# New SBUF addresses for three kinds of tiles in a fused attention, MLP and routed-expert kernel

## The chip, the cores and the metric

The kernel runs on one core of a Trainium2 chip. The metric is the device time of one execution in microseconds (us); lower is better. Matrix products run on TensorE (PE in the profile; its weight loads are the row PEld), which computes in turn with VectorE (DVE), ScalarE (ACT) and GpSimd (POOL); SyncE (SP) issues most transfers.

## The reference

Three stages follow one another, all in float32.

```
phi(x):  proj = x @ w_phi; proj -= max|proj|;  concat(exp(proj), exp(-proj))
attn  = (phi(q) @ (phi(k)^T v)) / (phi(q) @ sum phi(k) + 1e-6)    # 8 x 8 heads, 576 tokens, 64
x     = attn as 4608 tokens x 512
h     = x @ w_in;  x = (h * cos(h)) @ w_out                       # 512 -> 2048 -> 512
e     = argmax(x @ w_gate + modality_bias[modality_id]); p = its softmax weight
out   = p * (relu(x @ w1[e]) @ w2[e])                             # 8 experts, 512 -> 1024 -> 512
```

## The kernel before

**Attention** (lines 54 to 280) goes through 16 items of two batches by two heads, five groups each. Its products are L136 (projection), L174 (keys by values, the moving operand `v`) and L210 (numerator and denominator).

**The MLP** takes the tokens in 9 blocks `u` of 512 and, in each, 16 steps `f` of 128 hidden features. Each float32 operand is split into a high and a low part in the fp32r type, and a product is three matmuls (high by high, high by low, low by high). Step `f` issues 12 matmuls of 512 columns for the first layer (L473: stationary a 128x128 piece of the chunk `w0_f`, moving the tokens `x`) and then, three steps behind, 12 for the second (L511: stationary `gh` or `gl`, moving the chunk `w1_(f-3)`; in the last two blocks L516, with the roles exchanged). So steps 0, 1 and 2 of a block hold the second layer's chunks 13, 14 and 15 of the block before. The work around it is the cosine on ACT and DVE.

**The experts** take the sorted tokens in 18 slots of 256 and, after these, up to seven half slots of 128 (`half`, L799). A slot is 96 matmuls of 256 columns (L781: stationary the weight chunks `m0_f`, moving the turned tokens `xT_i`), then 48 of 512 columns (L793: stationary `hh` or `hl`, moving `m1_f` in even and `m2_f` in odd slots: 24 for each half of the tokens, three for each chunk `f`). In between lie transposes for the next slot (L766).

**Where tiles lie.** Tile pools are laid out one behind the other in each partition. The pool of the shared tiles (`SHARED`, a dictionary of floats per tile and number of tiles) comes early, then the pool `m_small` with the small tiles of routing and planning, then what lives in the attention alone; when the attention ends, the pool `late` takes that last place. `late` holds the 11 weight chunks that have no shared tile (tag `wl`, 4096 bytes each) and the tiles `x1T`. A chunk is a pair of halves, high and low, of 512 floats each, made by `pair`. The late chunks are `w0_12` to `w0_15` and `w1_9` to `w1_15`, and in the expert stage, in the same places, `m1_4` to `m1_7` and `m2_1` to `m2_7`. All other chunks, `m0` whole among them, lie in shared tiles.

The address of a tile is here its first byte within each partition, in the built program, and its remainder is that address modulo 512. The order of the work around the change is set by the code's own order and the planner of the tile framework.

Of the kernel before, what the change touches and what calls it, by code (L numbers as in the profile page):

```python
# [14 lines left out]
I32 = mybir.dt.int32  # L15
AF = mybir.ActivationFunctionType
ALU = mybir.AluOpType
AX = mybir.AxisListType
# [12 lines left out]

SHARED = {"raw_k":(1024,2),"raw_q":(1024,2),"ke":(1024,4),"qe":(1024,3),"xT":(1152,4),"xw":(1024,6),"kt":(512,3),"qt":(512,3),"kvh":(512,4),"kvl":(512,4),"kvt":(512,2),"wx":(1024,5),"sx":(1024,2)}

def shared_tiles(tc, ctx):
    sp=ctx.enter_context(tc.tile_pool(name="shared",bufs=1))
    def S(tag,name,dt=F32):
        w,n=SHARED[tag]
        return sp.tile([P,w],dt,tag=tag,name=name,bufs=n)  # L40
# [305 lines left out]
def moes(tc, ctx, consts, S, ps, ident, att, end_att, xt, w_in, w_out, x1d, tab, wgt, w1, w2, out):  # L346

    nc=tc.nc
# [8 lines left out]
    def xtile(tag,name,dt=F32R):  # L357
        if tag=="x1T": return late[0].tile([P,512],dt,tag="x1T",name=name,bufs=4)
        if tag=="row": return S(turn(("kvt","kvt","qt"),tag),name,dt)
        return S({"fr":"kt","n":"qt","gh":"kvh","gl":"kvl"}[tag],name,dt)  # L360
    def pair(tag,name):

        if tag=="wl": t=late[0].tile([P,1024],F32R,tag="wl",name=name,bufs=11)
        else: t=S(tag,name,F32R)
        return t[:,0:512],t[:,512:1024]
    pj=[]
    def bank(tag,name):
        if tag=="pj":
# [34 lines left out]
    def decoding(paced=False,steps=False):  # L403
# [7 lines left out]
        t=xtile("gl" if decoded[0]<=20 else "row",f"d_t{which}_{f}",F32)  # L411
        ti=t.bitcast(I32)
        h,l=pair(wtag[which][f],f"w{which}_{f}")
        (win,wout)[which][f]=(h,l)
        keep=tc.keep_in_program_order if paced else lambda ins: ins
# [43 lines left out]
    def split_x(u,d):  # L459
        if u>=NU: return  # L460
        r=xraw[u,d]
        h,l=pair("ke",f"x_{u}_{d}")
        nc.vector.tensor_copy(h,r)  # L463
        (nc.vector if d==3 else nc.gpsimd).tensor_tensor(l,r,f32(h),ALU.subtract)
        xhl[u,d]=(h,l)
# [62 lines left out]
    def load_gate():  # L528
        for tag in ("raw_k","raw_k","raw_q","kvt","kvt"):
            t=S(tag,f"wg_{len(wg)}")  # L530
            for j in range(SHARED[tag][0]//512):
                e=len(wg)
# [51 lines left out]
    def small(n,u,shape,dt=F32): return sb.tile(shape,dt,tag="s_"+n,name=f"{n}_{u}",bufs=1)  # L584
# [50 lines left out]
    o={}; e_={}; off_={}  # L635
    PRE=4; TAKE=64*T-8
    def key(n):

        t=small(n,0,[1,8])
        nc.vector.tensor_tensor(t,C["run"][0:1,:],C["base"][0:1,:],ALU.subtract)  # L640
        nc.vector.scalar_tensor_tensor(t,t,64.0,C["num"][0:1,:],op0=ALU.mult,op1=ALU.add)
        return t
    def value(ap,engines,hi,why): return nc.values_load(ap,engines=engines,min_val=0,max_val=hi,skip_runtime_bounds_check_because=why)
    SP=[mybir.EngineType.SP]
    def first():

        t0=t=key("k1")
        m=small("km",0,[1,PRE])
        for j in range(PRE):
            nc.vector.tensor_reduce(m[:,j:j+1],t,AX.X,ALU.max)  # L650
            h=small("kis",0,[1,8]); nc.vector.tensor_tensor(h,t,m[:,j:j+1].to_broadcast([1,8]),ALU.is_equal)
            n=small(f"kt{j}",0,[1,8]); nc.vector.scalar_tensor_tensor(n,h,-float(TAKE),t,op0=ALU.mult,op1=ALU.add)
            t=n
        o["took"]=small("took",0,[1,8]); nc.vector.tensor_tensor(o["took"],t,t0,ALU.subtract)
        mi=small("kmi",0,[1,PRE],I32); nc.vector.tensor_copy(mi,m)
        e=small("kme",0,[1,PRE],I32); nc.vector.tensor_scalar(e,mi,7,None,op0=ALU.bitwise_and)
        g=small("kmg",0,[1,PRE],I32); nc.vector.tensor_scalar(g,mi,56,None,op0=ALU.bitwise_and)
        ef=small("kef",0,[1,PRE]); nc.vector.tensor_copy(ef,e)
        gf=small("kgf",0,[1,PRE]); nc.vector.tensor_copy(gf,g)
        nc.vector.tensor_scalar(ef,ef,float(REG),None,op0=ALU.mult)  # L660
        of=small("kof",0,[1,PRE],I32)
        nc.vector.scalar_tensor_tensor(of,gf,T/8.0,ef,op0=ALU.mult,op1=ALU.add)
        o["pe"]=e; o["poff"]=of
    def order():


        t=key("k2")
        nc.vector.tensor_tensor(t,t,o["took"],ALU.add)
        srt=small("srt",0,[1,8]); nc.vector.max(srt,t)
        ki=small("ki",0,[1,8],I32); nc.vector.tensor_copy(ki,srt)  # L670
        ei=small("ei",0,[1,8],I32); nc.vector.tensor_scalar(ei,ki,7,None,op0=ALU.bitwise_and)
        gi=small("gi",0,[1,8],I32); nc.vector.tensor_scalar(gi,ki,56,None,op0=ALU.bitwise_and)
        n=small("on0",0,[1,16])
        for j,more in ((0,T//2-1),(1,T-1)):
            kj=small(f"ki{j}",0,[1,8],I32); nc.vector.tensor_scalar(kj,ki,64*more,None,op0=ALU.add)
            nc.vector.tensor_scalar(kj,kj,14,None,op0=ALU.logical_shift_right)
            nc.vector.tensor_copy(n[:,8*j:8*j+8],kj)
        nc.vector.tensor_tensor(n[:,8:16],n[:,8:16],n[:,0:8],ALU.subtract)

        b=small("ob",0,[1,17]); nc.vector.memset(b[:,16:17],0.0)  # L680
        nc.vector.tensor_scalar(b[:,0:8],ei,8.0*REG+1.0,None,op0=ALU.mult)
        gf=small("gf",0,[1,8]); nc.vector.tensor_copy(gf,gi)
        nc.vector.scalar_tensor_tensor(b[:,0:8],gf,float(T),b[:,0:8],op0=ALU.mult,op1=ALU.add)
        nc.vector.scalar_tensor_tensor(b[:,8:16],n[:,0:8],8.0*T,b[:,0:8],op0=ALU.mult,op1=ALU.add)
        end=small("on1",0,[1,16])
        nc.vector.tensor_tensor_scan(end,C["ones"],n,float(PRE),op0=ALU.mult,op1=ALU.add)
        db=small("db",0,[1,16]); nc.vector.tensor_tensor(db,b[:,1:17],b[:,0:16],ALU.subtract)
        nc.vector.scalar_tensor_tensor(db,n,-8.0*T,db,op0=ALU.mult,op1=ALU.add)
        ge=small("ge",0,[1,NS1,16])
        nc.vector.tensor_tensor(ge,C["slot"].unsqueeze(2).to_broadcast([1,NS1,16]),end.unsqueeze(1).to_broadcast([1,NS1,16]),ALU.is_ge)  # L690
        nc.vector.tensor_tensor(ge,ge,db.unsqueeze(1).to_broadcast([1,NS1,16]),ALU.mult)
        sv=small("sv",0,[1,NS1+8+16])[:,0:NS1]; nc.vector.tensor_reduce(sv,ge,AX.X,ALU.add)
        nc.vector.scalar_tensor_tensor(sv,C["slot"],8.0*T,sv,op0=ALU.mult,op1=ALU.add)
        iv=small("iv",0,[1,NS1],I32); nc.vector.tensor_scalar(iv,sv,b[:,0:1],-8.0*T*PRE,op0=ALU.add,op1=ALU.add)
        ie=small("ie",0,[1,NS1],I32); nc.vector.tensor_scalar(ie,iv,7,None,op0=ALU.bitwise_and)
        io=small("io",0,[1,NS1],I32); nc.vector.tensor_scalar(io,iv,3,None,op0=ALU.logical_shift_right)

        ni=small("ni",0,[1,3+NSH],I32)
        nc.vector.tensor_copy(ni[:,0:1],end[:,7:8]); nc.vector.tensor_copy(ni[:,1:2],end[:,15:16])
        h=small("oh0",0,[1,NSH]); nc.vector.tensor_scalar(h,C["slot"][:,NS0:NS0+NSH],end[:,7:8],None,op0=ALU.is_ge)  # L700
        h2=small("oh1",0,[1,NSH]); nc.vector.tensor_scalar(h2,C["slot"][:,NS0:NS0+NSH],end[:,15:16],None,op0=ALU.is_lt)
        nc.vector.tensor_tensor(ni[:,2:2+NSH],h,h2,ALU.mult)
        h3=small("oh2",0,[1,1]); nc.vector.tensor_scalar(h3,end[:,15:16],NS0+1.5,None,op0=ALU.is_gt)
        nc.vector.scalar_tensor_tensor(ni[:,2+NSH:3+NSH],end[:,7:8],NS0+0.5,h3,op0=ALU.is_lt,op1=ALU.mult)
        o.update(e=ie,off=io,n=ni)
# [5 lines left out]
    def alloc_w():  # L711

        for n in range(NF2):
            tag=wtag[1][n]
            t=late[0].tile([P,1024],F32,tag="wl",name=f"raw_{n}",bufs=11) if tag=="wl" else S(tag,f"raw_{n}",F32)
            RAW.append(t[:,0:1024])
        sets=[[pair(tags[f0+f],f"m{n}_{f}") for f in range(NF2)] for n,(tags,f0) in enumerate(((wtag[0],0),(wtag[0],NF2),(wtag[1],NF2)))]
        for i in range(NS1):
            W[i,0]=sets[0]; W[i,1]=sets[1+i%2]
# [23 lines left out]
    X={}  # L743
    R={}
    def alloc(i):
        X[i]=list(zip(*[pair("ke",f"xT_{i}_{g}") for g in range(2)]))
    xgs={}; spare=[]
    def alloc_g(i):
        R[i]=sb.tile([P,2,2],I32,tag="mrec",name=f"mrec_{i}",bufs=4)
# [141 lines left out]
    for F in range(3,NU*NF+LAG):  # L891
        step(F)
        if F==NF+1: load_gate()
        if F==(NU-1)*NF+3: first()
        if F==(NU-1)*NF+7:
            for i in range(2):
                alloc_g(i); load_off(i); gather(i)
        if F==(NU-1)*NF+11:
            for i in range(3): load_e(i)
            alloc_w()  # L900
            for m in (4,5,6,7,0,1,2,3): fetch(m)
            ws=itertools.chain(split_steps(0,0),split_steps(0,1))
        if F>(NU-1)*NF+12:
            pin.append(1)
            for _ in range(3): next(ws,None)
            pin.pop()
        if F==NU*NF+1: alloc(0); prep(0)
# [7 lines left out]
    def hooks(i,steps):  # L915
# [28 lines left out]
        if i==1:  # L944
            h[1].append(lambda: route2(u))
            h[4].append(order)
# [125 lines left out]
```

## Time and profile before

| | |
|---|---|
| median of 3 runs | 1647.42 us (1645.74 to 1648.21) |
| the profiled execution | 1647.8 us |
| its span, first to last instruction | 1645.6 us |
| PE busy | 1612.9 us, 98% of the span |
| DVE, ACT, POOL busy | 1152.3, 846.9 and 411.0 us |
| moved by DMA | 195.55 MB |

The profiled execution is 2.2 us longer than its span and 0.4 us above the median. Matmuls are pipelined: a matmul's own row shows the time from its start to its modelled end, which overlaps the next one, so what a matmul costs is read from the start of one to the start of the next.

### The profile page before, as it was taken

The numbers are of one execution on the slowest core, as the hardware profiler recorded it, in microseconds if no ns is written. First come the engines' busy times: TensorE is split into PE (matmuls) and PEld (weight loads), VectorE is DVE, ScalarE is ACT, GpSimd is POOL, SyncE is SP. The second block draws the span as 40 slices with busy tenths as digits, with TensorE's granted clock in tenths as the row PEclk, the third lists the DMA queues.
The fourth block names the chain that finished last, engine by engine and source line by source line (L and its number), as shares of the span: only waits on it lengthen the run. The fifth ranks groups of instructions, "written<-read, shape, count | busy, mean of one in ns | idle before, by whom it ended". The sixth has DMA issues, their size and how long they took to land. (4 is left out here: it accounts for less than half of the span.)

```text
span 1645.6 us, 33698 instructions
## 1 busy us (share of the span) xinstructions
PE 1612.9 (98%) x13076; PEld 1375.7 (84%) x13076; DVE 1152.3 (70%) x2364; ACT 846.9 (51%) x1563; POOL 411.0 (25%) x336
## 2 busy tenths in 40 slices
PE   8999999989999999999999999999999999999997
PEld 6888888878788888888888888888899899989985
DVE  5888888888766868586867677665875556565645
ACT  5677666656533434343433333344755555555645
POOL 0000000022123434333333333343112211111113
PEclk9999999999999999999999999999999999999999
DMA  6744444423210101010100101004758667766656
GB/s 170 224 136 137 139 138 140 136 94 125 82 45 14 39 7 45 7 39 14 39 13 21 31 7 39 8 14 146 246 140 314 218 222 244 251 216 214 215 190 234
DMA packets 144832, 195.55 MB, mean 119 GB/s; under 512 B 64648, under 2 KB 89352, under 8 KB 144659
## 3 DMA queue, kind: packets, MB, share of 16 engines
q1 hardware_dynamic: 136866, 172.24, 33.2%
q0 software_dynamic: 7792, 21.02, 3.8%
q8 instruction: 107, 1.75, 0.5%
q14 instruction: 67, 0.54, 0.1%
HBM read 162.18 MB, written 31.82 MB: 118 GB/s over the span
## 5 line engine op out<-in xcount | busy, mean ns | idle before, releaser
L473 PE MATMUL ph<-x,w 128*128 128x512 f32 x1728 | 425.0, 394 | 4.5 <-DVE x L463 3.3
L473 PEld LDWEIGHTS ph<-x,w 128*128 128x128 f32 x1728 | 323.4, 188 | 79.8 <-DVE x L463 4.4
L500 POOL TENSOR_TENSOR gl<-fr,gh 128x512 fp32r<-128x512 f32 x130 | 195.8, 1509 | 367.0 <-DVE gh L499 336.4
L740 DVE TENSOR_TENSOR m<-raw,m 128x512 fp32r<-128x512 f32 x320 | 207.9, 686 | 109.2 <-ACT m L739 109.0
L511 PE MATMUL acc<-w,gh 128*128 128x512 f32 x896 | 277.9, 391 | 0.0
L486 ACT ACTIVATE n<-ph 128x512 int32<-128x512 f32 x144 | 86.0, 597 | 263.7 <-PE ph L473 263.5
L781 PEld LDWEIGHTS mh<-xT,m 128*128 128x128 f32 x1728 | 210.0, 191 | 2.4 <-DVE hl L784 0.7
L781 PE MATMUL mh<-xT,m 128*128 128x256 f32 x1728 | 210.9, 283 | 0.5 <-DVE hl L784 0.5
L739 ACT CAST m<-raw 128x512 fp32r<-128x512 f32 x320 | 187.4, 618 | 42.9 <-PE mh L781 33.6
L511 PEld LDWEIGHTS acc<-w,gh 128*128 128x128 f32 x896 | 168.2, 188 | 36.9
L488 DVE SCALAR_TENSOR_TENSOR fr<-ph,n 128x512 f32<-128x512 f32 x144 | 99.1, 688 | 133.8 <-ACT n L486 117.6
L541 DVE SCALAR_TENSOR_TENSOR junk<-x1T,wg 128x512 f32<-128x512 f32 x224 | 183.0, 817 | 0.0
L793 PE MATMUL po<-m,hh 128*128 128x512 f32 x576 | 182.2, 397 | 0.0
L511 PE MATMUL acc<-w,gl 128*128 128x512 f32 x448 | 175.4, 392 | 0.0
L490 ACT ACTIVATE fr<-fr 128x512 f32<-128x512 f32 x144 | 91.1, 632 | 159.7 <-DVE fr L488 159.5
L493 DVE SCALAR_TENSOR_TENSOR fr<-fr,ph 128x512 f32<-128x512 f32 x144 | 98.6, 684 | 68.6 <-ACT fr L491 68.6
L793 PEld LDWEIGHTS po<-m,hh 128*128 128x128 f32 x576 | 105.5, 188 | 21.7
L793 PE MATMUL po<-m,hl 128*128 128x512 f32 x288 | 113.4, 394 | 0.0
L836 POOL DMA_INDIRECT out_dram<-o,mrec x39 | 42.5, 1089 | 282.3 <-ACT o L835 268.3
L511 PEld LDWEIGHTS acc<-w,gl 128*128 128x128 f32 x448 | 84.1, 188 | 18.5
L491 ACT ACTIVATE fr<-fr 128x512 f32<-128x512 f32 x144 | 90.9, 632 | 4.0
L141 DVE TENSOR_REDUCE m_q<-pj 128x4 f32<-128x512 f32 (+1 forms) x80 | 50.9, 637 | 57.7 <-PE pj L136 57.7
(215 smaller groups left out, 2391.0 us busy)
## 6 DMA issues: line engine op xcount, KB each, us to landing
raw<-in_moe_w_dram SPq DMA_DIRECT2D x170, 512.0 KB, 6.0
xt<-xo SPq DMA_DIRECT2D x16, 576.0 KB, 4.4
xr<-xt SPq DMA_DIRECT2D x36, 256.0 KB, 2.9
raw_k<-in_k_dram SPq DMA_DIRECT2D x32, 256.0 KB, 2.9
raw_q<-in_q_dram SPq DMA_DIRECT2D x32, 256.0 KB, 4.1
v<-in_v_dram SPq DMA_DIRECT2D x64, 128.0 KB, 3.4
st<-in_moe_w_in_dram SPq DMA_DIRECT2D x16, 512.0 KB, 4.1
st<-in_moe_w_out_dram SPq DMA_DIRECT2D x16, 512.0 KB, 3.9
```

The source lines that it names most:

```text
L473: nc.tensor.matmul(ph,A[:,ws],xhl[u,d][k],start=n[0]==0,stop=n[0]==11); n[0]+=1
L488: nc.vector.scalar_tensor_tensor(g,ph,INV2PI,n,op0=ALU.mult,op1=ALU.subtract)
L490: nc.scalar.activation(g,g,AF.Sin,scale=math.pi)
L491: nc.scalar.activation(g,g,AF.Square)
L493: nc.vector.scalar_tensor_tensor(g,g,-0.5,ph,op0=ALU.add,op1=ALU.mult)
L500: nc.gpsimd.tensor_tensor(gl,g,f32(gh),ALU.subtract)
L511: nc.tensor.matmul(accs[u][c],A[:,ws],B,start=(f==0 and k==0),stop=(f==NF-1 and k==2))
L541: return lambda: tc.keep_in_program_order(nc.vector.scalar_tensor_tensor(junk,x1T[u,c],1.0,wg[e],op0=ALU.mult,op1=ALU.mult,accum_out=lgs[u ...
L739: keep(nc.scalar.copy(h,a))
L740: keep(nc.vector.tensor_tensor(l,a,f32(h),ALU.subtract))
L781: nc.tensor.matmul(ph[:,f2*T:(f2+1)*T],A[:,ws],B[d//2][:,xs],start=n==0,stop=n==11); n+=1
L793: nc.tensor.matmul(po[c],A[:,ws],B,start=(f==0 and j==0),stop=(f==NF2-1 and j==2))
```

## The change

Three edits, none of which touches an instruction's kind, size or place.

```diff
-"ke":(1024,4)
+"ke":(1152,4)
...
-    def pair(tag,name):
+    def pair(tag,name,o=0):
...
-        return t[:,0:512],t[:,512:1024]
+        return t[:,o:o+512],t[:,o+512:o+1024]
...
-        e=small("kme",0,[1,PRE],I32); nc.vector.tensor_scalar(e,mi,7,None,op0=ALU.bitwise_and)
-        g=small("kmg",0,[1,PRE],I32); nc.vector.tensor_scalar(g,mi,56,None,op0=ALU.bitwise_and)
+        eg=small("kme",0,[1,2*PRE],I32); e,g=eg[:,0:PRE],eg[:,PRE:2*PRE]
+        nc.vector.tensor_scalar(e,mi,7,None,op0=ALU.bitwise_and)
+        nc.vector.tensor_scalar(g,mi,56,None,op0=ALU.bitwise_and)
...
-        sv=small("sv",0,[1,NS1+8+16])[:,0:NS1]; nc.vector.tensor_reduce(sv,ge,AX.X,ALU.add)
+        sv=small("sv",0,[1,NS1]); nc.vector.tensor_reduce(sv,ge,AX.X,ALU.add)
...
-        X[i]=list(zip(*[pair("ke",f"xT_{i}_{g}") for g in range(2)]))
+        X[i]=list(zip(*[pair("ke",f"xT_{i}_{g}",112) for g in range(2)]))
```

The tiles `ke` grow from 4096 to 4608 bytes, and the turned tokens `xT` begin 448 bytes into them; the MLP's tokens `x`, in the same tiles, still begin at their first byte. Two small tiles of the planning become one, and one loses 24 floats it did not use, which makes `m_small` 128 bytes shorter. The remainders of the addresses in the two built programs:

| tiles | before | after |
|---|---|---|
| shared tiles: chunks `w0_0` to `w0_11`, `w1_0` to `w1_8`, `m0`, `m1_0` to `m1_3`, `m2_0`; `x`, `gh`, `gl`, `hh`, `hl` | 320 | 320 |
| the 11 late chunks | 448 | 320 |
| turned tokens `xT` | 320 | 256 |
| `x1T` (loads of tokens, gathered tokens) | 448 | 320 |
| attention's `v`, in turn | 448, 32 | 320, 416 |
| attention's `qx`, `w2` | 256, 128 | 128, 0 |

The two programs hold the same 21,018 instructions in the same order, with the same waits. The one place where even a name differs is the planning's arithmetic on DVE, in the last block of the MLP (`kme`, `kmg`: the expert's number and its group, cut out of a packed key `kmi`; numbers at the ends of names count tiles):

```order
-L656 TENSOR_SCALAR kme_12391<-kmi_12389 1x4
-L657 TENSOR_SCALAR kmg_12393<-kmi_12389 1x4
+L657 TENSOR_SCALAR kme_12391<-kmi_12389 1x4
+L658 TENSOR_SCALAR kme_12391<-kmi_12389 1x4
 L654 TENSOR_TENSOR took_12387<-kt_0_12385,k_0_12363 1x8
```

Nothing moved there: the second of the two writes goes to the other half of the same tile.

## Rows read from the trace of the kernel before

**Rows 1.** Page, part 1: busy us, share of the span, instructions.

```profile
PE 1612.9 (98%) x13076; PEld 1375.7 (84%) x13076; DVE 1152.3 (70%) x2364; ACT 846.9 (51%) x1563; POOL 411.0 (25%) x336
```

**Rows 2.** Busy time by stage: attention, MLP, expert slots, half slots.

```profile
core 0: us, PE busy (x) PEld busy (x) DVE busy (x) ACT busy (x) POOL busy (x), PEclk, DMA share, GB/s
100.00:330.00 230.00, 223.85 (x4451) 203.71 (x4452) 189.52 (x452) 159.41 (x365) 15.48 (x22) 1.00 0.47 140
400.00:1160.00 760.00, 758.91 (x3407) 617.16 (x3406) 534.25 (x1111) 300.02 (x482) 270.52 (x191) 1.00 0.12 36
1196.10:1596.90 400.80, 400.29 (x2599) 363.67 (x2598) 239.48 (x410) 228.32 (x402) 75.36 (x70) 1.00 0.68 225
1600.00:1645.60 45.60, 36.16 (x172) 28.05 (x170) 25.88 (x42) 27.27 (x51) 14.54 (x7) 0.98 0.64 216
```

**Rows 3.** PE alone, block 4 of the MLP: steps 6 to 9, steps 12 to 15.

```profile
741.62:763.38 21.76, 21.76 (x97) 1.00 0.06 13
774.27:796.61 22.34, 22.34 (x97) 1.00 0.00 1
```

**Rows 4.** Timeline of PE in block 4: steps 2, 3 and 12 (start us, us).

```profile
719.28 2.90 PE L473 MATMUL ph<-x,w 128*128 128x512 f32 x12
722.01 0.62 PE L511 MATMUL acc<-w,gh 128*128 128x512 f32 x2
...
724.81 2.90 PE L473 MATMUL ph<-x,w 128*128 128x512 f32 x12
727.54 0.61 PE L511 MATMUL acc<-w,gh 128*128 128x512 f32 x2
...
730.26 0.20 PE L616 MATMUL pk<-ob,tri 128*128 128x8 bf16 x2
...
774.27 2.96 PE L473 MATMUL ph<-x,w 128*128 128x512 f32 x12
777.06 0.62 PE L511 MATMUL acc<-w,gh 128*128 128x512 f32 x2
...
779.84 2.95 PE L473 MATMUL ph<-x,w 128*128 128x512 f32 x12
```

**Rows 5.** Timeline of PE in expert slots 6 and 7 (start us, us).

```profile
1328.35 0.62 PE L793 MATMUL po<-m,hh 128*128 128x512 f32 x2
...
1331.14 0.63 PE L793 MATMUL po<-m,hh 128*128 128x512 f32 x2
...
1349.77 0.62 PE L793 MATMUL po<-m,hh 128*128 128x512 f32 x2
...
1354.64 0.64 PE L793 MATMUL po<-m,hh 128*128 128x512 f32 x2
```

**Rows 6.** PE alone while L781 runs, in slots 5, 7 and 8.

```profile
1290.55:1302.05 11.50, 11.50 (x97) 1.00 0.58 204
1337.56:1349.07 11.51, 11.51 (x97) 1.00 0.58 204
1361.11:1372.63 11.52, 11.52 (x98) 1.00 0.56 203
```

**Rows 7.** Timeline of PE in the attention: two bursts of L174 and what follows.

```profile
109.72 1.10 PE L174 MATMUL kv<-v,ke 128*64 128x65 f32 x32
110.76 0.44 PE L121 MATMUL pt<-ident,raw_q 128*128 128x128 f32 x2
...
130.59 1.10 PE L174 MATMUL kv<-v,ke 128*64 128x65 f32 x32
131.63 0.65 PE L121 MATMUL pt<-ident,raw_q 128*128 128x128 f32 x4
```

**Rows 8.** Page, part 5: groups of L739, L781, L210 and L136.

```profile
L781 PE MATMUL mh<-xT,m 128*128 128x256 f32 x1728 | 210.9, 283 | 0.5 <-DVE hl L784 0.5
L739 ACT CAST m<-raw 128x512 fp32r<-128x512 f32 x320 | 187.4, 618 | 42.9 <-PE mh L781 33.6 <-DMA raw<-in_moe_w_dram 3.0 <-PE po L793 0.9
L210 PE MATMUL pn<-kvz,qx 128*64 128x65 f32 x2304 | 85.2, 225 | 1.3 <-ACT xo L228 1.3
L136 PE MATMUL pj<-w,qT 64*128 64x128 f32 x576 | 54.6, 300 | 13.1 <-DVE rd L216 8.0 <-DMA w<-in_w_phi_dram 2.2 <-DVE t_k L142 1.4
L136 PE MATMUL pj<-w,kT 64*128 64x128 f32 x576 | 48.0, 276 | 0.0
```

More of the change, by code (lines that the diff above doesn't have):

```diff
@@ L30, in f32 @@
     return ap.bitcast(F32)
-SHARED = {"raw_k":(1024,2),"raw_q":(1024,2),"ke":(1024,4),"qe":(1024,3),"xT":(1152,4),"xw":(1024,6),"kt":(512,3),"qt":(512,3),"kvh":(512,4),"kvl":(512,4),"kvt":(512,2),"wx":(1024,5),"sx":(1024,2)}
+SHARED = {"raw_k":(1024,2),"raw_q":(1024,2),"ke":(1152,4),"qe":(1024,3),"xT":(1152,4),"xw":(1024,6),"kt":(512,3),"qt":(512,3),"kvh":(512,4),"kvl":(512,4),"kvt":(512,2),"wx":(1024,5),"sx":(1024,2)}
 def shared_tiles(tc, ctx):
```

## The prediction

> **What bounds the kernel now.** I read the page's busy times first: PE is busy for 98% of the span, the next engine for 70% [rows 1]. Then the same by stage: in the MLP and in the expert slots PE is busy for all but 1.1 us of 760 and 0.5 us of 401, at a granted clock of 1.00 of 2.4 GHz, while DVE has 70% and 60%, and the transfers take 12% and 68% [rows 2]. So in these two stages the time is the sum of the intervals at which PE starts one matmul after another. Only in the half slots at the end does PE idle, for 9 of 46 us [rows 2]. The change alters no instruction, no order and no wait, so the question is whether an interval depends on where the operands lie.
>
> It does, as the rows stand. Steps 6 to 9 of an MLP block, whose 96 matmuls have all operands at remainder 320, take 21.76 us: 226.7 ns each. Steps 12 to 15 have the same 96 matmuls, but the weight chunks of both layers are late ones at 448, and take 22.34 us: 232.7 ns each [rows 3]. Nothing waits in either: PE is busy for the whole stretch. Two things set the difference apart from the steps around it. In step 2 only the second layer's chunk is late: its half takes 724.81 - 722.01 = 2.80 us, where the first layer's half, from a shared chunk, takes 2.73, and in step 3, where the second layer is back at its chunk 0, its half takes 2.72 [rows 4]. In step 12 both halves are long, 2.79 and 2.78 us [rows 4]. So the extra goes with the chunk, whether it is the stationary operand (L473) or the moving one (L511). The expert slots say the same: 12 matmuls with `m1_4` to `m1_7` take 2.79 us in slot 6, and 21 with `m2_1` to `m2_7` take 4.87 us in slot 7, which is 231.9 ns each [rows 5].
>
> The Trainium skill, "SBUF — State Buffer", section "Who interferes with whom", has it that TensorE reads its moving operand and its weights through two independent ports and never waits on anyone. By that rule no address could matter to PE, and the time would stay. The trace does not agree: 226.7 against 232.7 ns for the same instructions [rows 3].
>
> **The change part by part.**
>
> *Late chunks from 448 to 320, in the MLP.* They come to the remainder that the shared chunks have, so I price their matmuls like those. Steps 12 to 15 give back 22.34 - 21.76 = 0.58 us a block [rows 3]. The second layer's halves of steps 0, 1 and 2 give back 2.80 - 2.72 = 0.08 us each [rows 4], 0.24 in all. That is 0.82 us a block and 7.4 us for nine; in the last two blocks the second layer has its operands exchanged, which I price the same, since both roles show the extra.
>
> *Late chunks in the expert slots.* 12 aligned matmuls cost 12 x 226.7 ns = 2.72 us, and an even slot has two stretches like the one of 2.79 us [rows 5]: 0.14 us. An odd slot has two of 21 matmuls at 4.87 against 4.76 us: 0.22 us. Nine slots of each: 9 x (0.14 + 0.22) = 3.2 us.
>
> *Turned tokens from 320 to 256.* All 1728 matmuls of L781 [rows 8] now read a moving operand 64 bytes off the remainder of their stationary one; until now both were at 320. They cost 11.51 us for 96, or 119.9 ns [rows 6]. No row shows a displacement of 64 bytes in these matmuls. Bounds: 256 more columns cost 226.7 - 119.9 = 106.8 ns, so a matmul of 256 columns has 13.1 ns on top of its columns. If the new place freed all of it, 1728 x 13.1 ns = 22.6 us would go; if it doubled, as much would come. The nearest row is the displacement of 128 bytes, at 232.7 - 226.7 = 6.0 ns: +10.4 us. My value is zero, half-way between these ends: three slots with different token tiles, and with different chunk sets before them, come out within 0.02 us [rows 6], which shows a settled rhythm, and 64 bytes are half of the one displacement whose price is known, in an unknown direction. In the half slots the tokens are stationary and displaced the other way, but PE idles there.
>
> *Everything else.* The tiles `ke` are longer by 512 bytes, which moves all behind them by 2048: remainders there stay. In the attention, `v`, `qx`, `w2` change place. Its L174 has had `v` at 448 and at 32 in turn: bursts of 32 take 1.04 us at 109.72 (448) and 1.04 us at 130.59 (32) [rows 7], so I price the attention at zero. The clock of these rows is 0.01 us, 1%; of the 188 us in L210 and L136 [rows 8], which have no such pair, that is 2 us either way, kept for the range. The planning's arithmetic on DVE has as many instructions as before. The transfers into `x1T` are as large as before, and in the MLP they take 12% of the DMA engines [rows 2]. Where PE gets faster, weights are asked for earlier: ACT's splitting (L739) has waited for weights 3.0 us in all [rows 8], and 0.2 us in a slot of 23.5 is 1% more demand on transfers at 68% [rows 2], so I charge nothing; without that cover the 3.2 us of the expert slots would not come.
>
> The sum is 7.4 + 3.2 = 10.6 us off the profiled execution's 1647.8 us, of which 2.2 lie outside its span. That execution is 0.4 us above the median of the runs, so from 1647.4 the forecast is 1636.8, rounded to 1637.0.
>
> **The rivals.**
>
> *The tokens' new place pays too* (20%). L781 loses part of its 13.1 ns, from 1.5 ns to half of it: 2.6 to 11.3 us more off, 1625.5 to 1634. For it: there is something to lose. Against: equal remainders are the best place that the rows show.
>
> *The tokens' new place costs, but less than the chunks give* (12%). From 1.5 to 6.0 ns, the price of 128 bytes: 1639.5 to 1647.
>
> *Slower: L781 pays a second stall* (5%). If 64 bytes doubled its extra, it would cost 22.6 us against 10.6: 1659.4. It decides from 10.6 us / 1728 = 6.1 ns for no change, and 8.0 ns for slower by over 0.2%. For it: L781 has the shortest matmuls, with a weight load at every 119.9 ns, so a stall has least room. Against: a displacement twice as large costs 6.0 ns.
>
> *It is not the remainder* (8%). The late chunks also lie highest in SBUF, and they come in the same steps each time; if height or neighbours make them slow, the chunks stay at 232 ns and the time stays at 1647.4 (tokens at zero). For it: no row has a late chunk at 320, or a shared one at 448. Against: nothing but PE works differently in step 2's two halves. The ports rule of the Trainium skill, cited above, would end in the same time for another reason.
>
> **How the numbers follow.** The forecast, chunks at 226.7 ns and L781 within 1.5 ns (2.6 us) of now, has 55%: 1634 to 1640. Of the range, the gain on L781 and the attention's 2 us reach down to 1628, the moderate loss up to 1645; outside lie the slower case, "not the remainder" and the far end of the gains, some 18%. A measurement of this kernel can tell about 0.2%, 3.3 us, from no change: faster means below 1644.1. Forecast, gain, and some 8 of the 12 points of the moderate loss lie there: 83%. The other 4 and the 8 of "not the remainder" make the same, 12%; slower is 5%.
>
> **What would show it.** Steps 12 to 15 of a block at 21.76 us instead of 22.34, and step 2's second half at 2.72; `m2_1` to `m2_7` at 4.76 us. L781's 96 matmuls at 11.5 us: at 11.0 the tokens pay, at 12.1 they cost as much as the chunks gave. L174's bursts at 1.04 us. The prediction is wrong if the late chunks stay at 232 ns, or if L781 moves by over 0.4 us a slot.

## The result, and the profile after

The changed kernel takes 1632.36 us (median of 6 runs, 1630.37 to 1635.49) where the kernel before takes 1646.58 (median of 6 runs): a ratio of 0.9917, with a 95% interval of [0.9906, 0.9927]. It is faster, by more than the 10.6 us of the sum. 1632.36 lies 4.6 us below the forecast of 1637.0 and below the 1634 to 1640 that had 55%; it lies within the range of 1628 to 1645, and in the 1625.5 to 1634 of the rival by which the tokens' new place pays too. In the changed kernel every line from 657 on has a number one higher, so L781, L793 and L739 are now L782, L794 and L740.

The page's busy times (part 1) show the same picture as [rows 1], with 14.3 us less of PE:

```profile
PE 1598.6 (98%) x13074; PEld 1370.5 (84%) x13076; DVE 1147.1 (70%) x2364; ACT 846.1 (52%) x1563; POOL 408.5 (25%) x336
```

The windows of the attention, of the MLP and of the expert slots are as full as in [rows 2]; columns as there:

```profile
100.00:330.00 230.00, 223.91 (x4449) 203.57 (x4447) 189.51 (x452) 159.22 (x364) 15.41 (x22) 1.00 0.48 140
400.00:1160.00 760.00, 758.53 (x3433) 620.69 (x3433) 534.16 (x1118) 304.48 (x493) 269.54 (x191) 1.00 0.13 37
1189.03:1582.20 393.17, 392.57 (x2598) 359.42 (x2597) 239.39 (x410) 228.27 (x402) 77.77 (x70) 1.00 0.69 230
```

Now the marks that the prediction set. PE in block 4, steps 6 to 9 and 12 to 15, against [rows 3]:

```profile
738.70:760.46 21.76, 21.76 (x97) 1.00 0.05 13
771.34:793.10 21.76, 21.76 (x97) 1.00 0.00 1
```

The steps with late chunks take what the others take. The timeline of step 2, against [rows 4], shows the second layer's half at 721.90 - 719.18 = 2.72 us:

```profile
719.18 0.62 PE L511 MATMUL acc<-w,gh 128*128 128x512 f32 x2
...
721.90 2.88 PE L473 MATMUL ph<-x,w 128*128 128x512 f32 x12
```

In slot 7, against [rows 5], `m2_1` to `m2_7` take 1344.55 - 1339.79 = 4.76 us:

```profile
1339.79 0.62 PE L794 MATMUL po<-m,hh 128*128 128x512 f32 x2
...
1344.55 0.62 PE L794 MATMUL po<-m,hh 128*128 128x512 f32 x2
```

The tokens' matmuls (L782) in slots 5, 7 and 8, against [rows 6], take 11.31 us for 96, 117.8 ns each, where 11.5 was said:

```profile
1281.63:1292.94 11.31, 11.31 (x98) 1.00 0.63 210
1327.80:1339.11 11.31, 11.31 (x97) 1.00 0.61 212
1350.89:1362.20 11.31, 11.31 (x98) 1.00 0.56 203
```

And a burst of L174, against [rows 7], takes 132.17 - 131.13 = 1.04 us, as before:

```profile
131.13 1.10 PE L174 MATMUL kv<-v,ke 128*64 128x65 f32 x32
132.17 0.66 PE L121 MATMUL pt<-ident,raw_q 128*128 128x128 f32 x4
```

The groups by line, against [rows 8], have L782 at 206.6 us of busy time, 4.3 less than before, and the attention's L210 and L136 within 0.3 us of where they were:

```profile
L782 PE MATMUL mh<-xT,m 128*128 128x256 f32 x1728 | 206.6, 281 | 0.6 <-DVE hl L785 0.6
L740 ACT CAST m<-raw 128x512 fp32r<-128x512 f32 x320 | 187.7, 619 | 39.7 <-PE mh L782 32.5
...
L210 PE MATMUL pn<-kvz,qx 128*64 128x65 f32 x2304 | 84.9, 224 | 1.3 <-ACT xo L228 1.3
L136 PE MATMUL pj<-w,qT 64*128 64x128 f32 x576 | 54.8, 302 | 12.5 <-DVE rd L216 8.1 <-DMA w<-in_w_phi_dram 1.7 <-DVE t_k L142 1.4
```

Where the time went is read from the first matmul of a stage to the first of a later one, in the traces before and after. From block 1 to block 8 the MLP takes 1057.64 - 439.26 = 618.38 us, before it took 1062.98 - 440.78 = 622.20: 3.8 us less, where the prediction's 0.82 us a block make 5.7. Timeline rows of both ends, after and then before:

```profile
439.26 1.07 PE L473 MATMUL ph<-x,w 128*128 128x512 f32 x4
...
1057.64 1.07 PE L473 MATMUL ph<-x,w 128*128 128x512 f32 x4
```

```profile
440.78 1.56 PE L473 MATMUL ph<-x,w 128*128 128x512 f32 x6
...
1062.98 1.31 PE L473 MATMUL ph<-x,w 128*128 128x512 f32 x5
```

From slot 2 to slot 17 the experts take 1559.36 - 1212.37 = 346.99 us, before 1573.42 - 1220.08 = 353.34: 6.4 us less, where 15 slots of the prediction's 0.18 us make 2.7. So the MLP gave less than forecast, and the experts more than twice as much. The first block is no basis: in two profiles of the same changed kernel it takes 87.2 and 88.6 us, and begins at 352.0 and 350.6.

### The profile page after: what moved, and what is told of

Same layout as the page of the kernel before. It is cut to its first block, busy times and chain, and to the rows that moved or that the text cites. A ratio compares the mean times of both kernels' runs of the same rounds, so it can differ in the third digit from the quotient of the medians.

```text
span 1630.7 us, 33696 instructions
## 1 busy us (share of the span) xinstructions
PE 1598.6 (98%) x13074; PEld 1370.5 (84%) x13076; DVE 1147.1 (70%) x2364; ACT 846.1 (52%) x1563; POOL 408.5 (25%) x336
## 4 chain that ended last, share of the span: by engine, by line
PE 72%; DVE 13%; ACT 6%; DMA 5%; issue 3%; POOL 0%; SPq 0%; DVEq 0%; POOLq 0%; ACTq 0%
PE ph L473 19%; PE acc L511 15%; PE mh L782 11%; PE po L794 10%; PE acc L516 4%; PE pj L136 4%; DMA out_dram<-o,mrec 3%; PE pn L210 2%; PE kv L174 2%; DVE x L463 2%; PE pt L121 1%; DVE t_k L142 1%; DVE m_k L141 1%; PE ptt L189 1%; DVE fr L488 1%
## 5 line engine op out<-in xcount | busy, mean ns | idle before, releaser
L473 PE MATMUL ph<-x,w 128*128 128x512 f32 x1728 | 422.6, 392 | 4.8 <-DVE x L463 3.7
L473 PEld LDWEIGHTS ph<-x,w 128*128 128x128 f32 x1728 | 322.3, 188 | 78.9 <-DVE x L463 6.4
L511 PE MATMUL acc<-w,gh 128*128 128x512 f32 x896 | 276.1, 389 | 0.0
L740 ACT CAST m<-raw 128x512 fp32r<-128x512 f32 x320 | 187.7, 619 | 39.7 <-PE mh L782 32.5
L782 PEld LDWEIGHTS mh<-xT,m 128*128 128x128 f32 x1728 | 205.6, 189 | 2.5 <-DVE hl L785 1.0
L782 PE MATMUL mh<-xT,m 128*128 128x256 f32 x1728 | 206.6, 281 | 0.6 <-DVE hl L785 0.6
L511 PEld LDWEIGHTS acc<-w,gh 128*128 128x128 f32 x896 | 168.2, 188 | 35.1
L794 PE MATMUL po<-m,hh 128*128 128x512 f32 x576 | 179.6, 393 | 0.0
L511 PE MATMUL acc<-w,gl 128*128 128x512 f32 x448 | 174.4, 389 | 0.0
L794 PEld LDWEIGHTS po<-m,hh 128*128 128x128 f32 x576 | 105.2, 188 | 19.6
L794 PE MATMUL po<-m,hl 128*128 128x512 f32 x288 | 112.4, 390 | 0.0
L511 PEld LDWEIGHTS acc<-w,gl 128*128 128x128 f32 x448 | 84.1, 188 | 17.5
```

The costliest lines, as they stand in the source:

```text
L473: nc.tensor.matmul(ph,A[:,ws],xhl[u,d][k],start=n[0]==0,stop=n[0]==11); n[0]+=1
L511: nc.tensor.matmul(accs[u][c],A[:,ws],B,start=(f==0 and k==0),stop=(f==NF-1 and k==2))
L740: keep(nc.scalar.copy(h,a))
L782: nc.tensor.matmul(ph[:,f2*T:(f2+1)*T],A[:,ws],B[d//2][:,xs],start=n==0,stop=n==11); n+=1
L794: nc.tensor.matmul(po[c],A[:,ws],B,start=(f==0 and j==0),stop=(f==NF2-1 and j==2))
```

## The experiments

"Distance" below means the remainder of the moving operand's address less that of the stationary operand's, modulo 512. An interval in ns is the mean from one matmul's start to the next one's, from the starts in the trace; for L473 over steps 5 to 11 of a block (seven steps of twelve), where nothing is waited for. The last block is left out: other matmuls (L561, L562) stand between its steps, and there L473 takes some 233 ns in every kernel that has it at distance 0, the kernel before too (233.3), for which no run here tells the cause.

**The two moves, each alone.** The first kernel is the changed one with the turned tokens back at the remainder of their weights, so it keeps the new places of `x1T` and of the attention's tiles; the second is the kernel before with only the tokens' tiles enlarged and moved, so that the late chunks stay at 448.

```diff
 # chunks alone, against the changed kernel
-        X[i]=list(zip(*[pair("ke",f"xT_{i}_{g}",112) for g in range(2)]))
+        X[i]=list(zip(*[pair("ke",f"xT_{i}_{g}",0) for g in range(2)]))
 # tokens alone, against the kernel before
-"ke":(1024,4)
+"ke":(1152,4)
...
+    def pair(tag,name,o=0):
...
+        return t[:,o:o+512],t[:,o+512:o+1024]
...
+        X[i]=list(zip(*[pair("ke",f"xT_{i}_{g}",112) for g in range(2)]))
```

> The changed kernel with the turned tokens back at the first byte of their tiles (remainder 320), the late chunks at 320. Theory: the two edits are independent, each worth what the changed kernel's trace shows, so the chunks alone give the step intervals (226.7 ns for a matmul of 512 columns) and L782 returns to 120.0 ns: 1728 x 1.9 to 2.2 ns = 3.3 to 3.8 us slower than the changed kernel, about 1636, ratio to before 0.994. Rival: the tokens' place does nothing by itself and L782 got faster because the expert slots around it lost their displaced chunks; then this run equals the changed kernel, 1632.4, with L782 at 118.1 ns.

> The kernel before with the tiles ke at 4608 bytes and the turned tokens 448 bytes into them; the late chunks stay at remainder 448. Theory: L781 at 117.8 to 118.1 ns instead of 120.0, the displaced chunks as slow as before (232 to 233 ns): 3.8 us faster than before, about 1642.8, ratio 0.998. Rival (the tokens' place does nothing by itself): 1646.6 and L781 at 120.0 ns.

Chunks alone: 1638.46 us, ratio 0.9952 [0.9936, 0.9969]. Tokens alone: 1641.72 us, ratio 0.9976 [0.9967, 0.9986]. Multiplied they give 0.9928, the whole change 0.9917: within the intervals two gains that add up, by these ratios of 7.9 us (5.1 to 10.5) and 3.9 us (2.3 to 5.4) of some 1646. The chunks alone came out 2.5 us slower than the 1636 that was expected. In the windows, chunks alone have slot 7's L782 at the old 11.52 us and steps 12 to 14 of block 4 at 16.32 = 3 x 5.44:

```profile
1328.91:1340.43 11.52, 11.52 (x98) 1.00 0.62 206
...
770.12:786.44 16.32, 16.32 (x74) 1.00 0.00 1
```

Tokens alone have the steps at 16.76, and L782 faster in slots 5, 7 and 8:

```profile
1287.45:1298.33 10.88, 10.88 (x98) 1.00 0.61 215
1333.21:1344.52 11.31, 11.31 (x98) 1.00 0.60 205
1356.57:1367.87 11.30, 11.30 (x97) 1.00 0.55 200
...
774.16:790.92 16.76, 16.76 (x74) 1.00 0.00 1
```

Slot 5's 10.88 us, 113.3 ns a matmul, was expected by nobody. Slots 2, 4 and 6 of this run have it too, at the same addresses as slots 7 and 8.

**A coarse sweep.** One kernel in which the distance grows by 64 bytes from slot to slot and from block to block, up to 448; all weights stay where the change puts them.

```diff
-        h,l=pair("ke",f"x_{u}_{d}")
+        h,l=pair("ke",f"x_{u}_{d}",16*(u%8))
...
-        X[i]=list(zip(*[pair("ke",f"xT_{i}_{g}",112) for g in range(2)]))
+        X[i]=list(zip(*[pair("ke",f"xT_{i}_{g}",16*(i%8)) for g in range(2)]))
```

> The changed kernel with the tokens placed 64 x (i mod 8) bytes into their tile in expert slot i, and the MLP's tokens x 64 x (u mod 8) bytes into theirs in block u: one execution that shows all eight displacements of the moving operand against its stationary one, for 256 and for 512 columns. Theory (an extra that depends on the distance of the two addresses modulo some power of two): 120.0 ns at 0, 117.8 at 448, 120.0 at slot 8 and 16 again; at 128 and 384 in the MLP about 232 ns as the late chunks had, at 448 less than 226.7. If the distance counts modulo 256, offsets 256, 320, 384, 448 repeat 0, 64, 128, 192. Rival (only the absolute alignment of the moving operand to 256 bytes counts, which 448 reaches with remainder 256): 192 and 448, that is remainders 0 and 256, are the fast ones and all others equal.

It takes 1646.88 us in one execution. The intervals of L473 (512 columns) by distance:

```
distance      0       64      128      192      256      320      384      448
ns        226.67   230.29   232.63   233.33   226.67   230.27   232.64   233.33
```

The price repeats after 256 bytes, and 0 is the best place of the eight; the gain that was expected at 448 did not come. The windows of L782 (256 columns) in slots 10 to 14, at distances 128, 192, 256, 320 and 384, go the other way: 11.51 at the multiples of 128, 11.31 between them. The rival by which only 192 and 448 are fast falls, since 320 is as fast as 192.

```profile
1408.78:1420.30 11.52, 11.52 (x98) 1.00 0.58 207
1432.12:1443.43 11.31, 11.31 (x98) 1.00 0.61 205
1455.21:1466.72 11.51, 11.51 (x97) 1.00 0.61 208
1478.53:1489.84 11.31, 11.31 (x98) 1.00 0.57 202
1501.66:1513.17 11.51, 11.51 (x97) 1.00 0.63 206
```

Here the shared chunks, which are neither late nor highest in SBUF, are slow as soon as the tokens are displaced. So the rival "it is not the remainder" falls.

**Everything 128 bytes further.** The changed kernel behind one unused tile of 32 floats: chunks, tokens and `gh` then lie at 448, the very remainder at which the late chunks were slow, with all distances kept.

```diff
+    cpool.tile([P, 32], F32, name="shift")
```

> The changed kernel with one unused tile of 128 bytes ahead of the shared pool, so that every operand of the three stages moves by 128 bytes: chunks, x, gh and gl at 448 instead of 320, the turned tokens at 384 instead of 256. Theory (only the distance between the operands counts): as the changed kernel, steps of 5.44 us and L782 at 118 ns, 1632 to 1633. Rival (the remainder 448 itself is slow, or 320 fast): MLP steps of 5.58 us and more, over 1640.

It takes 1630.83 us in one execution, and the windows of block 4's steps 6 to 9 and of slot 7's L782 are those of the changed kernel:

```profile
737.34:759.10 21.76, 21.76 (x98) 1.00 0.05 13
...
1326.38:1337.69 11.31, 11.31 (x97) 1.00 0.62 207
```

So neither the remainder 320 or 448 nor alignment to 256 or 512 counts; the distance does. A shift of 128 bytes keeps every alignment to 128 bytes or less, so it can't tell the distances that are no multiple of 128 from such an alignment; no run here tests that.

**Which load it is.** The changed kernel with the experts' tokens at distance 0 and with only `gl` and `hl` 128 bytes further on. They are the stationary operand of each third matmul of L511 and L794.

```diff
 # two of the four edits; the others put the tokens back to 0 and their tiles to 4096 bytes
-"kvl":(512,4)
+"kvl":(640,4)
...
-        return sp.tile([P,w],dt,tag=tag,name=name,bufs=n)
+        return sp.tile([P,w],dt,tag=tag,name=name,bufs=n)[:,32*(tag=="kvl"):w-96*(tag=="kvl")]
```

> The changed kernel with all operands of the 512-column matmuls at one remainder, and only the small halves gl and hl (the stationary operand of every third matmul of L511 and L794) 128 bytes further on; tokens of the experts back at 320. Of three matmuls the sequence of stationary operands is then 0, 0, 128 against the moving one at 0. Theory A (a matmul's moving reads collide with the load of the next matmul's weights, which runs beside it): the second matmul of three is the slow one, 232.7 ns, the first and third stay at 226.7. Theory B (the matmul's own two operands collide): the third is slow. Both: L511's 12 of a step take 4 x 6.0 = 24 ns more, 2.74 instead of 2.72 us, and the kernel about 0.024 x 112 + 288 x 0.006 = 4.5 us more than with the chunks alone, so 1642 to 1643. Rival C (one slow neighbour sets a new rhythm for all): all three at 230 ns or more.

It takes 1644.99 us in one execution, more than the 1642 to 1643 of either theory. L511's intervals by place among three: 226.9 ns (`gh` with `gh` next), 232.5 (`gh` with `gl` next), 234.1 (`gl` with `gh` next). Theory A explains the second, theory B the third, and neither alone explains both: a matmul is slow if its own weights lie off, and also if the next ones do. The second layer's half of a step shows it in the timeline: 723.15 - 720.37 = 2.78 us, where either theory alone gave 2.74.

```profile
720.37 0.62 PE L511 MATMUL acc<-w,gh 128*128 128x512 f32 x2
...
723.15 2.88 PE L473 MATMUL ph<-x,w 128*128 128x512 f32 x12
```

**Finer sweeps.** Two kernels like the coarse one: distances in steps of 16 bytes over the slots and 32 over the blocks; and then the odd multiples of 16 over the blocks, with 112, 16 and 240 in turn over the slots.

```diff
 # fine
+        h,l=pair("ke",f"x_{u}_{d}",8*u)
+        X[i]=list(zip(*[pair("ke",f"xT_{i}_{g}",4*i) for g in range(2)]))
 # odd places
+        h,l=pair("ke",f"x_{u}_{d}",4+8*u)
+        X[i]=list(zip(*[pair("ke",f"xT_{i}_{g}",(28,4,60)[i%3]) for g in range(2)]))
```

> The changed kernel, with the turned tokens moved by 16 bytes more in each of the 18 expert slots (0 to 272 bytes from the remainder of their weights) and the MLP's tokens by 32 bytes more in each of the nine blocks (0 to 256). Theory (the interval depends on the distance of the two operands modulo 256, and the coarse sweep has seen its extremes): L473 at 226.7 ns in blocks 0 and 8, about 228.5 at 32 bytes, 230.3 at 64, then up to 233.3 at 192 and down again at 224 bytes; L782 at 120.0 ns at distances 0, 128 and 256, 117.8 at 64 and 192, and between the two in between. Rival (what counts is a step of 64 bytes, a line or a bank): 16, 32 and 48 bytes give either the value at 0 or the value at 64, with nothing in between. Second rival (there is a better place between the coarse steps): some slot under 117 ns, or some block under 226 ns, by over 0.5 ns.

> The changed kernel with the experts' tokens 112, 16 and 240 bytes from the remainder of their weights, in slots 0, 3, 6.., 1, 4, 7.. and 2, 5, 8..; and the MLP's tokens at the odd multiples of 16 bytes that the sweep left out: 16, 48, 80, 112, 144, 176, 208, 240 and 272 in blocks 0 to 8. Theory (a distance sets a rhythm, the same each time): the slots at 112 bytes take 10.92 us each for the 96 matmuls of L782, as slot 7 of the fine sweep (113.7 ns), those at 16 bytes 11.1 (115.2), those at 240 bytes 11.25 (117.2). Rival (several rhythms are possible at one distance, and what ran before chooses): slots with the same distance differ by over 0.1 us. In the MLP, theory: no block below 226.7 ns, since none of nine others was; rival (the good places of the 512-column matmuls are odd multiples of 16 bytes too): a block at 220 ns, which would be 1.3 us a block in L473 alone.

They take 1647.2 and 1641.5 us in one execution each. L473 has no better place than 0: 231.4 ns at 16 bytes, 233.6 at 32, 233.4 at 48, 230.3 at 64, 234.6 at 96, 230.3 at 112. It isn't smooth, and the expected 228.5 at 32 bytes was wrong. L782 does have a better place: 10.92 us for 96 at 112 bytes, or 113.7 ns. The windows of slots 6 to 8 of the fine sweep, at 96, 112 and 128 bytes:

```profile
1316.36:1327.89 11.53, 11.53 (x98) 1.00 0.62 205
1339.71:1350.63 10.92, 10.92 (x98) 1.00 0.60 217
1362.44:1373.95 11.51, 11.51 (x97) 1.00 0.55 201
```

The second kernel repeats it: slots 3, 6, 12 and 15 all have 10.92, those at 16 bytes 11.39 (11.1 was expected), those at 240 bytes 11.25. From slot 2 on, in slots without a wait, each distance tried more than once in the sweeps gives one value, to 0.02 us; only 192 has shown two (10.9 and 11.31, above).

**The tokens at 112 bytes.** The changed kernel with the offset 28 instead of 112 floats.

> The changed kernel with the experts' tokens 112 bytes from the remainder of their weights instead of 192 (28 floats into the tile instead of 112). Theory (113.7 ns holds in all slots): 18 x (11.31 - 10.92) = 7.0 us less than the changed kernel, 1625.4, ratio to the kernel before 0.987 to 0.988. Rival (slot 7 of the sweep was one chance rhythm of several): some slots 10.9, others 11.5, the time between 1626 and 1633. Second rival (where the slots get shorter, the experts' weights come late): L782 at 10.92 a slot, but idle time of PE in slots 1 to 17 grows by the same, and the time stays at 1632.

It takes 1630.35 us, ratio 0.9901 [0.9884, 0.9917]. L782 takes 10.92 us in all but two of the slots 2 to 17 that don't wait, and 10.96 and 11.03 in these two. But the gain is smaller than 7 us, and from this run alone it can't be told from the changed kernel. From slot 0 to the last L794 the trace is 4.4 us shorter: the waits in slots 0 and 9 grew.

**The wait in step 0.** Why did the MLP give back so little? In blocks 2 to 7 steps 1, 2 and 5 to 15 take 5.44 us each after the change, but step 0 takes 6.05 to 6.12 us, where it took 5.90 to 5.92 (in block 1 7.65 against 7.06). In the changed kernel's timelines around block 2 (PE, then DVE) the second layer of step 14 begins at 520.35, step 15 at 523.07, block 2 at 528.51, and step 1 at 534.62, 6.11 us later. The four casts of the new tokens (L463) take 4.71 us and end at 529.76, 1.25 us into step 0:

```profile
520.35 0.62 PE L511 MATMUL acc<-w,gh 128*128 128x512 f32 x2
...
523.07 2.88 PE L473 MATMUL ph<-x,w 128*128 128x512 f32 x12
528.51 3.50 PE L473 MATMUL ph<-x,w 128*128 128x512 f32 x12
534.62 0.61 PE L473 MATMUL ph<-x,w 128*128 128x512 f32 x2
```

```profile
524.10 0.43 DVE L499 CAST gh<-fr 128x512 fp32r<-128x512 f32 x1
...
525.05 4.71 DVE L463 CAST x<-xr 128x512 fp32r<-128x512 f32 x4
529.79 1.66 DVE L464 TENSOR_TENSOR x<-xr,x 128x512 fp32r<-128x512 f32 x1
```

VectorE has no idle time before these casts (no bracket stands behind them): they come in its own order, behind its work for step 14, and begin 525.05 - 520.35 = 4.70 us after that step's first half. The trace before has the same 615.34 - 610.64 = 4.70 us, here around block 3 (PE, then DVE):

```profile
610.64 0.63 PE L511 MATMUL acc<-w,gh 128*128 128x512 f32 x2
...
619.03 3.28 PE L473 MATMUL ph<-x,w 128*128 128x512 f32 x12
```

```profile
615.34 4.71 DVE L463 CAST x<-xr 128x512 fp32r<-128x512 f32 x4
```

What covers this work and the casts is three halves of steps, and that is 528.51 - 520.35 = 8.16 us now, where it was 619.03 - 610.64 = 8.39. The casts take as long as before, so they end 0.2 us later in step 0. The mean of 4.71 / 4 = 1.18 us mixes two durations (minimum, median and maximum in ns):

```profile
L463 DVE CAST x<-xr x4: 415/1508/1512, 525.0 to 528.2; 128x512 fp32r<-128x512 f32 x4
```

Three of the four take 1.51 us, each begun while a subtraction of GpSimd runs. The other, begun at 526.48 between two of them (one ends at 526.27, the next begins at 526.63), takes 0.42 us, as the cast of L499 ahead of them takes 0.43. So it is with all 36 of this run: the 23 that begin while an instruction of GpSimd runs take 1.50 to 1.51 us, the other 13 take 0.41 to 0.42. The Trainium skill, "SBUF — State Buffer", section "Who interferes with whom", has it that a cast on VectorE can contend with GpSimd for a port pair that the two share, while ScalarE has ports of its own; 1.51 against 0.42 us agrees. So the next kernel moves these casts to ScalarE from block 1 on, where it is mostly idle.

```diff
-        nc.vector.tensor_copy(h,r)
+        (nc.scalar.copy if u>0 else nc.vector.tensor_copy)(h,r)
```

> The changed kernel with one thing more: from block 1 on the four casts of the MLP's tokens (L463) run on ScalarE instead of VectorE; addresses as in the changed kernel. Theory (part of the chunks' gain is given back because step 0 of blocks 1 to 8 waits for these casts, which take 1.18 us each beside GpSimd's subtractions): step 0 falls from 6.12 us towards 5.44, at most 8 x 0.68 = 5.4 us, so 1627 to 1631, ratio to the kernel before 0.988 to 0.991. Rival (the wait passes on to the subtractions on GpSimd, L464, and to the last one on VectorE, which are as late): step 0 stays above 5.9 us and the time at 1632. Second rival (ScalarE's casts delay its own activations of step 15): the second layer of step 15 or step 0 gets longer, and the time rises above 1633.

It takes 1632.50 us, ratio 0.9922 [0.9903, 0.9941]: no gain in time. Yet step 0 falls to 5.77 us in blocks 2 to 7 (5.66 in block 8), and slot 0 begins 3.6 us earlier, 1.0 us of it because the MLP began earlier (351.04 against 352.04). Three casts take 1.98 us on ACT and the fourth 0.61 (its timeline, same place; the bracket is ACT's idle time, here until PE has read the old tokens from these tiles):

```profile
522.75 1.98 ACT L463 CAST x<-xr 128x512 fp32r<-128x512 f32 x3 [0.68 <-PE ph L473]
...
525.29 0.61 ACT L463 CAST x<-xr 128x512 fp32r<-128x512 f32 x1
```

The gain goes in the expert slots. In slot 9 of the changed kernel ACT waits 1.48 us for the weights' transfer and PE then 0.60 us (in brackets, ACT and PE):

```profile
1373.56 1.66 ACT L740 CAST m<-raw 128x512 fp32r<-128x512 f32 x3 [1.48 <-DMA raw<-in_moe_w_dram]
...
1380.39 1.87 PE L782 MATMUL mh<-xT,m 128*128 128x256 f32 x14 [0.60 <-DVE hl L785]
```

With the casts on ACT it waits 2.82 us, and PE 1.57:

```profile
1372.22 2.19 ACT L740 CAST m<-raw 128x512 fp32r<-128x512 f32 x4 [2.82 <-DMA raw<-in_moe_w_dram]
...
1378.69 1.54 PE L782 MATMUL mh<-xT,m 128*128 128x256 f32 x11 [1.57 <-DVE hl L785]
```

Over the whole run PE's waits in L782 for `hl`, which stands behind these splits on DVE, grow from 0.6 to 2.4 us. From slot 0 to the last L794 this run takes 423.88 us, the changed kernel 421.96: of the 2.6 us that the MLP gained, 1.9 are given back.

**Both additions, and the changed kernel again.** Tokens at 112 bytes and the casts on ScalarE, beside the changed kernel once more.

> The changed kernel with both things that gained in the trace: the experts' tokens 112 bytes from the remainder of their weights, and the casts of the MLP's tokens on ScalarE from block 1 on. Theory (each takes its time from a stage that PE bounds; part of it comes back as waits for weights in slots 0 and 9): slot 0 begins 3 us earlier than in the changed kernel, each settled slot takes 22.73 instead of 23.09 us, slots 0 and 9 wait 2 to 3 us more in all: 1632.4 - 3 - 6 + 3 = about 1626, ratio to the kernel before 0.986 to 0.989. Rival (the transfers of the weights now set the end of the expert slots, so what is gained before slot 9 is all lost there): slot 9 starts as late as in the changed kernel, and the time is 1629 or more.

> The changed kernel itself once more, beside the version that has both additions, on the same chip and against the same runs of the kernel before: 1632.4 within 2 us, ratio 0.991 to 0.993. L782 at 117.8 ns in the settled slots, late steps of the MLP at 5.44 us. If the version with both additions lies below it by more than the two intervals, that version is the better one; otherwise it can't be told.

Both additions: 1627.68 us, ratio 0.9881 [0.9866, 0.9896]. The changed kernel again: 1635.54 us, ratio 0.9931 [0.9917, 0.9945], whose interval overlaps the first one; the median is 3.2 us more than the first, where 2 us were expected at most. The first interval overlaps neither of the changed kernel's two, so this version is the faster one. It gains in both stages: slots 2 to 17 take 1553.66 - 1212.10 = 341.56 us, with PE busy all but 0.3 us of it, where the changed kernel beside it has 347.27, and blocks 1 to 7 take 616.2 against 618.3. But slot 0 begins only 0.6 us earlier, where 3 were expected, since the MLP begins 1.7 us later in this profile (352.31 against 350.62). Slot 9's wait, 0.62 against 0.93 us in L782's longest interval, was not longer here; why it was in the run with the casts alone stays open.

```profile
1212.10:1553.66 341.56, 341.22 (x2281) 1.00 0.71 238
```

## Why the prediction was right, and where it was not

*PE's intervals bound the two stages, and they depend on where operands lie.* Right: windows stay as full, and the time goes with the intervals. The rule of the Trainium skill, "SBUF — State Buffer", section "Who interferes with whom", that TensorE's two read ports are independent, by which no address should matter to PE, disagrees with all sweeps: 226.67 against 233.33 ns for the same matmul, the first as in [rows 3].

*Late chunks in the MLP, 7.4 us.* The mechanism was right to 0.01 us: 21.76 us and 2.72 us. The term was too large by what came after it. Of 0.82 us a block some 0.2 came back in step 0 (0.6 in block 1), for which the prediction has no term: PE reached the wait for the new tokens earlier, and VectorE's casts did not get faster. Blocks 1 to 7 gave 3.8 instead of 5.7 us. That the casts set a good part of this wait is shown by moving them: step 0 fell from 6.1 to 5.77 us. What is left above 5.44 the profile puts down to the subtractions of the new tokens (L464) on GpSimd.

*Late chunks in the expert slots, 3.2 us.* Right. Chunks alone take 1563.01 - 1212.35 = 350.66 us from slot 2 to slot 17, 2.7 us less than before, as 15 slots of 0.18 us.

*Turned tokens, zero.* This is the step that failed: "My value is zero, half-way between these ends". Measured alone they give 3.9 us, and 0.21 us a slot in the trace, 2.1 ns of each of 1728 matmuls. The bounds held, but the reasons for the middle did not. That three slots agreed showed a rhythm at distance 0 and nothing about the next one, and the price of 128 bytes in matmuls of 512 columns says nothing on matmuls of 256: there 128 bytes cost nothing (11.51 us a slot), and 64 bytes gain. The rival "the tokens' new place pays too" came true, at 3.9 us, the low end of its 2.6 to 11.3; its argument, that 13.1 ns were there to lose, was the better one, and its counter-argument, that equal remainders are the best place, holds for 512 columns only.

*Attention, zero.* Nothing shows otherwise: L174's bursts stay at 1.04 us, and the MLP's beginning varies by 1.4 us between two profiles of one kernel.

So by the ratios two errors of opposite sign stand in the sum: 10.6 - 7.9 = 2.7 us too much for the chunks, 3.9 us too little for the tokens. That they cancel to 1.2 us is luck. Of the 4.6 us by which the forecast missed these 1.2 are one part; 0.8 more are the kernel before, at 1647.42 when the forecast was made and 1646.58 over six runs, and 0.2 the rounding. The other 2.4 stay open; two medians of the changed kernel differ by more, by 3.2 us (1632.36 and 1635.54).

## What to carry to other kernels

Where PE is busy throughout, divide a full window by its matmuls, and compare stretches that differ only in where operands lie: a few ns of each can be had without touching an instruction. Give the operands of 512-column matmuls addresses that are equal modulo 256, but measure 256-column ones by themselves, with a kernel that changes the distance from stage to stage: one run shows all of them. And before booking a gain in one stage, look up what PE meets next, here casts and a transfer that don't come as much earlier as PE does.

## What the runs showed of the hardware

A matmul's interval depends on the distance between its moving operand and the weights loaded around it, and not on where both lie, as far as a shift of all by 128 bytes shows: at 512 columns 226.67 ns at 0 and 256, and 230.3 to 234.6 at all others tried; at 256 columns 119.9 ns at 0 and 128, 117.8 at 64 and 192, and 113.7 at 112. On VectorE the cast of a 128x512 tile of the tokens took 1.51 us when begun while GpSimd had an instruction running, and 0.42 us otherwise. The Trainium skill, "TensorE: Matmul & The Clock Gate", section "Wait — 56ns, not 53.3ns?", gives back-to-back matmuls at the full clock, from start to start, their columns at 2.4 GHz and about 2.5 ns more; as an estimate from that page this would be 215.8 and 109.2 ns, and no place tried here comes to it: the nearest are 226.67 and, in tokens alone, 113.3. What in the chip makes the distance count, and why distance 192 has shown two values, 113.3 and 117.8 ns, no run here tells.
